# Pooled attention with a maxout feed-forward: batch 1's queries in two parts, a fourth place for K and V, and a new order

## The chip, the cores and the metric

One core of one Trainium2 chip. The metric is device time in microseconds (us), the median over runs of the whole program. Inside the core five engines work from queues of their own: PE (TensorE, matmuls and transposes), DVE (VectorE), ACT (ScalarE), POOL (GpSimd) and SP (SyncE, which here issues DMAs). Each runs its queue in order, and semaphores hold an instruction back until others have ended.

## The reference

```python
# q, k, v: [8, 8, 1152, 64] fp32; w1, w2: [512, 1024]; w_out: [1024, 512]
q_pool = q.reshape(B, H, S // 2, 2, D).mean(axis=3)        # 576 queries per head
scores = scale * np.matmul(q_pool, k.transpose(0, 1, 3, 2))
attn = softmax(scores)                                     # over 1152 keys
x = np.matmul(attn, v).transpose(0, 2, 1, 3).reshape(B * 576, 512)
g = np.maximum(x @ w1, x @ w2)
out = g @ w_out                                            # [4608, 512] fp32
```

## The kernel before

**Algebra.** The maximum is written as relu(x(w1 − w2)) + x w2. So the kernel keeps `wd` = w1 − w2, `w21` = w2 w_out and `wo` = w_out in bf16, computes h = relu(x wd) and adds p = x w21 + h wo. All matmuls are in bf16 with fp32 sums.

**Pairs and blocks.** Two heads of a batch are a *pair*: 32 pairs, four per batch. A *block* is a pair and a range of its queries. Batch 0 comes in two parts: the first 256 queries of its four pairs (below called 0A to 3A), then the other 320. From batch 1 on a block is a whole pair of 576 queries.

**One pair** goes through these steps, named by line of the profile:

- K: load (L464, SP), cast to bf16 in `kbf` (L507, POOL, two buffers), transposed into `kT`: by PE (L518) and a DVE copy (L524) for pairs below `K_PE` = 5, else by a DMA on SP (L533, `ktrans`).
- V: load (L483, SP), cast into `vE` (L584, POOL).
- Q: load (L473, SP), the two neighbours added (L540, POOL, into `qp`), transposed into `qpT`: by PE (L554) with a DVE copy (L560) for pairs below `Q_PE` = 5, else by eight DVE transposes (L573).
- Scores: a score group is 512 columns of two heads (L598, PE), and ACT takes the exponential into `et` (L615).
- AV: chunks of 128 queries (L638) and a rest of 64 (L649) on PE; the V tile carries a column of ones, so the sum comes along.
- Norm: DVE takes the reciprocal of the sum (L661) and multiplies it in (L665, L670) into `xnat`.
- x is transposed into `xT`: by DMA on SP (L704, `xtrans`; two DMAs a pair) or by PE (L721) with a DVE copy (L726) for batch 0 and the pairs in `XPE`.

**Feed-forward.** When x of all four pairs of some tokens is there, h is computed in segments of tokens given by `CUTS` (L809 in pairs of column blocks, L788 singly near the end), and p in 256 tokens (L868; L888 singly at the end). A pair of matmuls on the two halves of PE's rows is called a duo. DVE copies p to `stage` and SP stores it (L829 to L845).

**Places.** K and V of a pair lie in a place, `slot(i)`. Batch 0's four pairs use places 0 to 3, the fourth of which lies in a tile (`xnat[1]`) that batch 1 needs itself; all later pairs go round three places:

```python
def slot(i):
    return i if i < NHP else (i - NHP) % 3
```

`stage` (L381) first holds the fp32 copies of w1 (lower half, later `gT`, the h results) and w_out (`wof`, upper half). Of the upper half the first part is used again as the output buffers `osb`; the rest is not used again once `wof` is cast to `wo`.

**Order.** `table()` holds the order of all engines, written out: one letter per PE unit (the letter is the PSUM bank, a capital letter is a filler of four matmuls on ones, L455, that feeds nobody) and lists of operation numbers for ACT, DVE, POOL and SP. `Plan.arrange` puts the operations in that order, `Plan.solve` works out which semaphore each must wait for. The order in which the main loop creates them only gives them their numbers.

Of the kernel before, what the change touches and what calls it, by code (L numbers as in the profile page):

```python
# [7 lines left out]
P = 128  # L8
# [172 lines left out]
def table():  # L181

    pe = (
        "AAAAAAAAAAAAAAAAAaBbaceGGGGGGGGGgAAacHhgeFfagcefAAAageeeecadegfcefagceageeeeccacecgafgcaedgacaaegabc"
        "cceaccgehcacccggcecccggaggggccegcacceaeeegecdeaeecgdeaggggceeeaeeegeeccaegcccaeeegeaeeecgccccacccecc"
        "cgcccccaeaagaaaaaecccaggegggaggggegggagggecccaggeccccageggggcaaaeggcaaaaegcgggaaeggggcaaaaeaaaagggcg"
        "ggggeaacgaaaaeccccagcccceaagccceccagccccecccaccccccccgcccecagaaeaacaagaaecgaeeeeeecgeeeacaaagaaaaecc"
        "cgcaeccccgaaaeaaacaggeggcaaeaagcaaeaagggcegaaacaaagaeeecageeeeecgeaaaceeeeaeeeegaaaeceeeaeeeeagaaeee"
        "ceaeeeeagaaaceeeegaceeeeegaggggcgggegggagccccgeggggaggccccegggcaceccaccceccaggecccacgcecccagggegggga"
        "cccegaccccccegeeaeeegeecacccgcccceaaagceaaaaaagcggeggggcgggaggecggggagggcgggaggeceeeeaeeegeeeceeeaee"  # L190
        "eegeeeceeaaaaaaaaagceeeeeeagceeeaaaagaaaaeceeegeeeeacaaagaaaaeceeegeeeeaacgeaaaaaaacggegggcgaaaageaa"
        "aagcgggaeeeegceeeeggagggeccccaecccccagegccccgaccccggeggcacccecccgaaaaegaaaaaecgcccceaaaacagaaaccecca"
        "gaaaeaaaagccceccccagggeggacggggeaaacagaeaaacgggeggggcaaaaegcaaaaaegeeeceeeeagggcgggeggagcgggegggaggg"
        "gcgggggeeeacgeeeeeeacaaeaaaagccccegccccceagaaaacaaaaeaaagccccaeccccagaaaceeeegaceeeeegaggggcggeaeeeg"
        "eeceeggaggeeecegeeeaegggcgggeggggagccecccageccccaaaagaaaaccecccacccgggeacggggggeaeeceeeeaggggcggggae"
        "eecegggageggcggeeaeeeceeeegeeeacccgeaccccccgegggcggggaaecgaaaaaaaeccgccaeccccgaaaeaaacaggeggggcgggag"
        "ggeggggcgggagggeggcacceggggaggggaaaccceaaaacccgeaaaaacgeggggcggggegggcaaaaecgggggagggggggeeeeeeeeeee"
        "ecccccccccaaaaaaaaaabaaeeeeeeeeeeeegggghhhhccccddddbbbbaaaahhhhddddggggaaaabbbbbbbbbaaaaeeeeffffaaaa"
        "eeeeffffaaaaeeeeffffaaaaeeeeffffaaaaeeeebbbaaaaaaaaaaaabbbbbbbbbbbbaaaaaaaaaaaabbbbbbbbbbbbaaaaaaaaa"
        "aaa"  # L200
    )
    act = (
# [17 lines left out]
    )  # L220
    dve = (
# [25 lines left out]
    )  # L247
    pool = (
# [5 lines left out]
    )  # L254
    sp = (
# [785 lines left out]
```

## Time and profile before

| | before |
|---|---|
| runs shown | 414.05, 414.01, 407.39 us (median 414.01) |
| profiled execution | 408.94 us, of it the span 407.2 us |
| mean granted TensorE clock | 0.971 |
| PE busy | 371.3 us, 91% of the span |
| ACT busy | 313.8 us, 77% |
| DVE busy | 236.5 us, 58% |
| POOL busy | 131.5 us, 32% |
| score groups, AV matmuls, fillers | 1142 matmuls (L598), 2232 + 558 (L638, L649), 136 (L455) |
| HBM | 62.91 MB read, 9.44 MB written |

How to read it: the span runs from the first to the last instruction of one profiled execution. Busy time is that of an engine's own instructions; waiting, branching and DMA issue are not counted. `SPq` rows are SP's queue: the time an issue took there. A view that lists waits names the engine and line that waited, and what released it. In a timeline, the number in brackets is the idle time of the engine just before the row.

### The profile page before, as it was taken

The page shows a single profiled execution, that of the slowest core. Times are in us where ns is not written, and L with a number is a line of the kernel's source. Part 1 is how long each engine was busy: PE and PEld are TensorE (multiplying, and loading weights), DVE is VectorE, ACT ScalarE, POOL GpSimd, SP SyncE. Part 2 cuts the span into 40 slices and gives each one's busy share as a digit, 9 for nine tenths or more (in the row PEclk, how much of TensorE's full clock was granted, in tenths as well). Part 3 has the DMA queues.
Part 4 walks back from the last instruction along what each step waited for, and adds up shares of the span by engine and source line. Part 5 has one row for each costly group of instructions (what it writes and reads, how often), then busy time and mean ns, then how long its engine had stood idle before and what let it go on. Part 6 is the DMA issues. An engine that isn't in the chain of part 4 may idle for free.

```text
span 407.2 us, 13616 instructions
## 1 busy us (share of the span) xinstructions
PE 371.3 (91%) x6061; PEld 234.8 (58%) x6064; DVE 236.5 (58%) x539; ACT 313.8 (77%) x359; POOL 131.5 (32%) x121
## 2 busy tenths in 40 slices
PE   8989999999689999999269994999699999999996
PEld 8756655675436655656136661566366666556573
DVE  1267549999639667874317672796177774243330
ACT  1599889999769999997239993999689999964231
POOL 2689483443613331234323033333323302000000
PEclk9999999999989999999759998999989999999999
DMA  7999999999996998987986969998966524023313
GB/s 262 400 404 392 377 241 333 329 274 320 280 322 126 244 176 184 227 185 182 270 232 168 210 157 247 224 211 269 196 171 129 132 58 90 13 57 67 78 27 104
DMA packets 79996, 85.19 MB, mean 209 GB/s; under 512 B 51905, under 2 KB 52673, under 8 KB 79937
## 3 DMA queue, kind: packets, MB, share of 16 engines
q1 hardware_dynamic: 79376, 83.53, 77.8%
q8 instruction: 47, 0.77, 0.8%
q10 hardware_dynamic: 560, 0.79, 0.5%
q14 instruction: 13, 0.10, 0.1%
HBM read 62.91 MB, written 9.44 MB: 178 GB/s over the span
## 4 chain that ended last, share of the span: by engine, by line
PE 80%; issue 5%; ACT 4%; DMA 4%; SPq 3%; POOL 2%; DVE 2%; POOLq 0%
PE ps L598 17%; PE ps L638 17%; PE ps L868 17%; PE ps L809 14%; ACT et L615 4%; DMA xT<-xnat 4%; PE ps L888 4%; PE ps L455 3%; PE ps L649 3%; PE ps L788 2%; PE ps L772 2%; SPq L704 1%; POOL qp L540 1%; DVE qpT L573 1%; POOL vE L584 1%
## 5 line engine op out<-in xcount | busy, mean ns | idle before, releaser
L615 ACT ACTIVATE et<-ps 128x1024 bf16<-128x1024 f32 (+5 forms) x340 | 305.4, 1009 | 60.4 <-PE ps L598 59.5
L598 PE MATMUL ps<-qpT,kT 64*128 64x256 bf16 (+7 forms) x1142 | 116.4, 287 | 1.7 <-ACT et L615 0.7
L573 DVE STREAM_TRANSPOSE qpT<-qp 32x288 bf16<-32x288 bf16 x216 | 101.3, 469 | 14.7 <-PE ps L598 10.1
L809 PE MATMUL ps<-xT,wd 64*128 64x256 bf16 (+3 forms) x704 | 79.2, 330 | 27.3 <-DMA xT<-xnat 26.2
L507 POOL TENSOR_SCALAR kbf<-kraw 128x1152 bf16<-128x1152 f32 (+1 forms) x32 | 36.4, 1139 | 160.2 <-DMA kT<-kbf 144.2
L638 PE MATMUL ps<-vE,et 128*128 128x65 bf16 x2232 | 81.2, 193 | 0.0
L638 PEld LDWEIGHTS ps<-vE,et 128*128 128x128 bf16 x2232 | 71.7, 97 | 13.0 <-issue 11.8
L815 DVE TENSOR_SCALAR stage<-ps 128x512 bf16<-128x512 f32 (+3 forms) x44 | 39.9, 907 | 63.8 <-PE ps L809 63.3
L598 PEld LDWEIGHTS ps<-qpT,kT 64*128 64x128 bf16 x1142 | 47.3, 95 | 46.1 <-ACT et L615 16.3
L868 PE MATMUL ps<-wo,stage 64*128 64x512 bf16 x480 | 69.4, 380 | 0.0
L809 PEld LDWEIGHTS ps<-xT,wd 64*128 64x128 bf16 x704 | 31.9, 98 | 52.7 <-DMA xT<-xnat 27.9
L540 POOL TENSOR_TENSOR qp<-qraw 128x576 bf16<-128x576 f32 (+2 forms) x35 | 44.8, 1285 | 18.5 <-DVE qpT L573 17.9
L584 POOL TENSOR_SCALAR vE<-vraw 128x1152 bf16<-128x1152 f32 x31 | 35.7, 1154 | 30.4 <-PE ps L638 30.4
L868 PE MATMUL ps<-w,xT 64*128 64x512 bf16 x240 | 35.5, 377 | 0.3 <-PE ps L809 0.3
L868 PEld LDWEIGHTS ps<-wo,stage 64*128 64x128 bf16 x480 | 23.1, 95 | 17.8 <-issue 0.7
L875 DVE COPY stage<-ps 128x1024 f32<-128x1024 f32 x15 | 18.3, 1221 | 19.3 <-PE ps L868 19.1
L661 DVE RECIPROCAL rc<-ps 128x5 f32<-128x5 f32 (+2 forms) x72 | 13.2, 183 | 27.8 <-PE ps L638 27.2
L670 DVE TENSOR_TENSOR xnat<-ps,rc 128x256 bf16<-128x256 f32 (+1 forms) x72 | 28.2, 394 | 1.9
L649 PEld LDWEIGHTS ps<-vE,et 128*64 128x64 bf16 x558 | 11.3, 111 | 10.2 <-issue 5.3
L868 PEld LDWEIGHTS ps<-w,xT 64*128 64x128 bf16 x240 | 10.6, 94 | 8.8 <-PE ps L809 0.5
L899 ACT COPY stage<-ps 128x512 f32<-128x512 f32 (+1 forms) x4 | 2.2, 560 | 17.3 <-PE ps L888 17.3
L649 PE MATMUL ps<-vE,et 128*64 128x65 bf16 x558 | 14.7, 197 | 0.7 <-ACT et L615 0.5
(50 smaller groups left out, 179.2 us busy)
## 6 DMA issues: line engine op xcount, KB each, us to landing
vraw<-in_v_dram SPq DMA_DIRECT2D x32, 576.0 KB, 6.1
kraw<-in_k_dram SPq DMA_DIRECT2D x31, 576.0 KB, 6.2
qraw<-in_q_dram SPq DMA_DIRECT2D x28, 576.0 KB, 6.1
out_dram<-stage SPq DMA_DIRECT2D x21, 256.0 KB, 4.2
out_dram<-stage SPq DMA_DIRECT2D x23, 128.0 KB, 3.4
xT<-in_moe_w_dram SPq DMA_DIRECT2D x4, 512.0 KB, 11.0
stage<-in_moe_w_dram SPq DMA_DIRECT2D x4, 512.0 KB, 11.8
stage<-in_moe_w_out_dram SPq DMA_DIRECT2D x4, 512.0 KB, 13.0
```

The source lines that it names most:

```text
L507: op("POOL", lambda g: g.tensor_scalar(dst, src, 1.0, 1.0, ALU.mult, ALU.mult), cost=0.02 + 0.126 * (hi - lo), **io)
L540: op(eng, lambda e: e.tensor_tensor(qp[s][:, lo:hi, :], qraw[z][:, lo:hi, 0, :], qraw[z][:, lo:hi, 1, :], ALU.add), r=[f"qraw{z}.{u}" for ...
L573: op("DVE", lambda e, src=src, dst=dst, pb=pb, db=db: e.transpose(view[dst:dst + 32, :, 32 * pb:32 * pb + 32], qp[s][src:src + 32, :, 32 * ...
L584: op("POOL", lambda g: g.tensor_scalar(vE[s][:, :, :, 0:D].rearrange("p t h d -> p h t d"), vraw[z][:, :, :, :], 1.0, 1.0, ALU.mult, ALU.m ...
L598: last = e.matmul(wide[m // 2][:, h, col:col + hi - lo], kT[slot(i)][rows(h), t, :], qpT[i % 4][rows(h), lo:hi], start=True, stop=True)
L615: op("ACT", lambda e, m, col=col, at=at, n=n: e.activation(et2[:, :, at:at + n], wide[m // 2][:, :, col:col + n], EXP, scale=scale), r=[f" ...
L638: last = e.matmul(fb[m + half][:, c * 66:c * 66 + 65], et[:, a:a + P], vE[s][:, t, half, 0:65], start=(t == 0), stop=(t == NT - 1))
L649: last = e.matmul(fb[m][rows(half), NCH * 66:NCH * 66 + 65], et[:, a:a + NB], vE[s][:, t, half, 0:65], start=(t == 0), stop=(t == NT - 1))
L670: op("DVE", lambda e, m: e.tensor_tensor(xnat[xs][:, hp, c0:c1, half * D:half * D + D], banks(m)[:, c0:c1, 0:D], rc[:, i, half, c0:c1].uns ...
L809: last = e.matmul(fb[m + k][:, 0:size], wd[z, ct, (f0 + k) * P:(f0 + k + 1) * P], xT[z, ct, n0:n1], start=(turn == 0 and ct == 0), stop=(t ...
L815: op("DVE", lambda e, m: e.tensor_scalar_max(gT[:, f0:f0 + 2, g0:g0 + size], wide[m // 2][:, :, 0:size], 0.0), r=[f"b{j}.0", f"b{j}.1"], w ...
L868: last = e.matmul(fb[m + k][:, :], lhs, rhs, start=(turn == 0 and x == 0), stop=(turn == 1 and x == NC_ + NF - 1))
```

## The change

- Batch 1 comes in two parts too (`blocks`, L413 of the new file): 256 queries of pairs 4 to 7, then 320. There are 40 blocks in place of 36. The loads, sums and transposes of these queries are cut in the same way, `xtrans` takes a range, and `place`, `spot` and `gkeys` put batch 1's tokens in the order in which they come.
- `Q_PE` goes from 5 to 8: the queries of pairs 5 to 7 are transposed by PE with a DVE copy, and no longer by DVE. 24 of 216 DVE transposes go.
- `XPE` has pair 7 besides pair 31: its x is transposed by PE.
- A fourth place for K and V of batch 1 and later, in the part of `stage` where the copy of w_out lay. The pairs go round four places. What writes there first waits until `wof` is cast.
- `CUTS` has 576 and 832 in place of 512.
- `home`, where a block's exponentials lie in `et`, is a written list for the first 16 blocks.
- `table()` is new in whole. Fillers go from 34 groups to 10 (136 to 40 matmuls). On SP the transposes of K, those of x, loads and stores stand in another order against each other, and so do h, p, score and AV units on PE.

```diff
 def table():
     pe = (
-        "AAAAAAAAAAAAAAAAAaBbaceGGGGGGGGGgAAacHhgeFfagcefAAAageeeecadegfcefagceageeeeccacecgafgcaedgacaaegabc"
...
+        "AAAAAAAabaceGGGgachgefagcefageeeceeagfecdfacegacaaaaeggcaaebggcgeahccccgeagcgbgeacgggegaaaaeeacaaaeeg"
...
-    K_PE, Q_PE, XPE = 5, 5, (NPAIR - 1,)
+    K_PE, Q_PE, XPE = 5, 8, (2 * NHP - 1, NPAIR - 1)
...
+        late = stage[:, (NC_ + 2) * F:2 * NC_ * F].bitcast(BF16)
+        kT.append(late[:, 0:NT * P].rearrange("p (t x) -> p t x", x=P))
+        vE.append(late[:, 2 * F:2 * F + NT * 132].rearrange("p (t h d) -> p t h d", h=2, d=66))
...
-            return i if i < NHP else (i - NHP) % 3
+            return i if i < NHP else (0, 1, 2, 4)[i % NHP]
...
-        blocks = [(i, 0, QA) for i in range(NHP)] + [(i, QA, SQ) for i in range(NHP)] + [
-            (i, 0, SQ) for i in range(NHP, NPAIR)]
+        EARLY = 2 * NHP
+        blocks = [(i, lo, hi) for b in range(2) for lo, hi in ((0, QA), (QA, SQ))
+                  for i in range(b * NHP, b * NHP + NHP)] + [(i, 0, SQ) for i in range(EARLY, NPAIR)]
...
-            home.append(i * NT * QA if hi == QA else i % 3 * NT * (SQ - QA) if hi - lo < SQ else (i + 1) % 2 * PW)
+        home = [0, 2304, 4608, 6912, 0, 2880, 5760, 0, 2880, 5184, 7488, 0, 2304, 5184, 0, 7488] + [
+            i % 2 * PW for i in range(EARLY, NPAIR)]
...
         def ktrans(i):
...
-                dma=f"d_kT{z}", cost=1.0, kind="ktrans", prio=i)
+                after=["wof2"] * (z == 4), dma=f"d_kT{z}", cost=1.0, kind="ktrans", prio=i)
...
         def place(b, c):
+            if b == 1:
+                return SQ + (c * P if c < 2 else NB + c * P if c < NCH else QA)
...
-        def xtrans(i):
+        def xtrans(i, lo, hi):
             b, ct = divmod(i, NHP)
-            spots = [(0, NCH, place(b, 0), P), (NCH, NCH + 1, place(b, NCH), NB)]
-            for c, z, n0, n in spots if b % 2 == 0 else spots[::-1]:
+            spots = [(c, z, place(b, c), P) for c, z in (((0, 2), (2, NCH)) if b == 1 else ((0, NCH),))
+                     if lo <= c * P < hi]
+            if hi == SQ:
+                spots.append((NCH, NCH + 1, place(b, NCH), NB))
+            for c, z, n0, n in sorted(spots, key=lambda x: x[2]):
...
+                if ct == NC_ - 1:
+                    op("POOL", lambda g: g.memset(vE[4][:, :, :, 64:66], 1.0), w=["vE4"],
+                       after=["wof2", "wof3"], fence=True, cost=0.1, kind="ones", prio=ct)
...
-        CUTS = (0, 256, 512, 1024, 1152, 1664, 2048, 2304, 2816, 3072, 3456, 3968, 4096, 4352, 4608)
+        CUTS = (0, 256, 576, 832, 1024, 1152, 1664, 2048, 2304, 2816, 3072, 3456, 3968, 4096, 4352, 4608)
```

More of the change, by code (lines that the diff above doesn't have):

```diff
@@ L183, in table @@
     pe = (
-        "AAAAAAAAAAAAAAAAAaBbaceGGGGGGGGGgAAacHhgeFfagcefAAAageeeecadegfcefagceageeeeccacecgafgcaedgacaaegabc"
[L185 to L198, printed above, removed]
@@ L199, in table @@
-        "eeeeffffaaaaeeeeffffaaaaeeeeffffaaaaeeeebbbaaaaaaaaaaaabbbbbbbbbbbbaaaaaaaaaaaabbbbbbbbbbbbaaaaaaaaa"
-        "aaa"
+        "AAAAAAAabaceGGGgachgefagcefageeeceeagfecdfacegacaaaaeggcaebggcgeahccccgeagcgbgeacgggegaaaaeeacaaaeeg"
+        "eeeeaacegaaagcccceccccabgceaggggaceccccgcccaeccacccgccceaegeeeccccgaeeeeeceeegaeeeceeeeaegggcggggaef"
+        "cghefagceeeeaaeaageccccaagaacaeaaaccgccaecccacccgccceaaagcceacgccceaagaaecaggaegggcaaaeaaaacagggeggc"
+        "aaaeaaaacaggggeggggacccegccaaeaaagaacceccacccgcaaaeacagaaaeeeeaeeeceaaagaaaecagggeggaccccgeccccaggge"
@@ new lines, in table @@
+        "cccacgcccecgggaceggggggacaaeaaaacggggaeggggaacagaeaaaaaaaacaaageeecageeeecaeeggggcggggeeeeaeeeeggggc"
+        "ggggeeeeaeeeeggggcegggggaceccccacccgegggcggggcaccgggegcggggcaccccgcccecccaggggeagggggceeeeaeeeegggcg"
+        "egagggeceeaeeeegcccacceggaccceggacgegggcaaaaeagacaaeeeeegaceeeegggagggcgggegggaggggcgggegggacccceacc"
+        "cccegagccceccccgcccaccegeeecaeeeecgcccaccceccccgaaaaegcaaaaaeegeeaaceeeegaaacaeaagggcaaaaeaaaacgggea"
+        "gggcecccacccgeeeecaeeeeccgcceacccgccccccccecaaagecaaaaaageggacgggegggaaaaaceaaaacgggeaaaagcaaaageggg"
@@ new lines, in table @@
+        "accccgcecccggagggceeeagceeeeeeagcccccccceaaaagaaacaeegeeeeceeeaggggcagggggceaeeggcggegagggceeeaeeegc"
+        "ccccagccccaeeegeeaccccgcccecaagaaeaaaacggggecagggggeceeeeaeeeceeegeaeceeeegeeeceeegeaaacaaagaaaecccc"
+        "geaacccccgeaacaaggggagggegaaacaaagaeeeecgaaaaeeeeecgaaaaeeeeceeeeaaagaaaaeaccccgccccaeeeegcaeeeeegcg"
+        "gggagggeccccacccceggggacggeggggagggccccegaccccceaggcccceccccgagggeggggccaecccccccgaeeeecgeeeeacccgcc"
+        "ceaaagaaaaeaaagaacaeaaagacaeaaagggggceaaaggggceaaaagcaaaaegggcgggageeeecagggggcggggagggceeeeeagggggg"
@@ L201, in table @@
+        "ggggggccccccccccccecccccccccccceeeeeeeeaaaaabaaaabbbbgggghhhhccccddddbbbbeeeeffffgggghhhhbbaaacccccc"
+        "cbbddddaaaabbbbddddaaaabbbbddddaaaabcccccdddddbbbaaaaccccbbbbaaaadddddddccccccccccccddddddddddddcccc"
+        "ccccccccdddddddddddd"
     )
     act = (
[17 rows of a table removed]
[17 rows of a table added]
     )
     dve = (
[25 rows of a table removed]
[26 rows of a table added]
     )
     pool = (
[5 rows of a table removed]
[6 rows of a table added]
     )
     sp = (
[11 rows of a table removed]
[12 rows of a table added]
     )
     bank_a = (
[5 rows of a table removed]
[5 rows of a table added]
     )
     bank_b = (
-        "1 44 454 459 463 473 483 "
+        "1 25 44 83 471 472 477 483 486 491 494 497 "
     )
     bank_c = (
[5 rows of a table removed]
[5 rows of a table added]
     )
@@ L285, in table @@
     bank_d = (
-        "34 38 83 84 458 462 "
+        "35 476 484 487 492 489 499 501 "
     )
     bank_e = (
[5 rows of a table removed]
[5 rows of a table added]
     )
     bank_f = (
-        "28 27 56 19 25 468 471 476 479 "
+        "28 27 34 19 130 76 479 "
     )
     bank_g = (
[4 rows of a table removed]
[5 rows of a table added]
     )
     bank_h = (
-        "14 59 456 461 "
+        "14 38 68 474 482 "
     )
@@ L400, in slot @@
         def slot(i):
-            return i if i < NHP else (i - NHP) % 3
-        blocks = [(i, 0, QA) for i in range(NHP)] + [(i, QA, SQ) for i in range(NHP)] + [
-            (i, 0, SQ) for i in range(NHP, NPAIR)]
+            return i if i < NHP else (0, 1, 2, 4)[i % NHP]
+        EARLY = 2 * NHP
+        blocks = [(i, lo, hi) for b in range(2) for lo, hi in ((0, QA), (QA, SQ))
+                  for i in range(b * NHP, b * NHP + NHP)] + [(i, 0, SQ) for i in range(EARLY, NPAIR)]
         NBL = len(blocks)
-        flat0, home = [], []
-        for n, (i, lo, hi) in enumerate(blocks):
-            flat0.append(flat0[-1] + NT * (blocks[n - 1][2] - blocks[n - 1][1]) if n else 0)
-            home.append(i * NT * QA if hi == QA else i % 3 * NT * (SQ - QA) if hi - lo < SQ else (i + 1) % 2 * PW)
+        home = [0, 2304, 4608, 6912, 0, 2880, 5760, 0, 2880, 5184, 7488, 0, 2304, 5184, 0, 7488] + [
+            i % 2 * PW for i in range(EARLY, NPAIR)]
+        flat0 = [NT * sum(hi - lo for _, lo, hi in blocks[:n]) for n in range(NBL)]
         NGR = (flat0[-1] + PW) // W
@@ L528, in ktrans_pe @@
                 op("DVE", evac, r=[f"b{j}.0"], w=[f"kT{z}.{t}" for t in range(lo, hi)], job=j,
-                   cost=0.16 + (hi - lo) * 0.067, kind="kev", prio=i)
+                   after=["wof2"] * (z == 4), cost=0.16 + (hi - lo) * 0.067, kind="kev", prio=i)
         def ktrans(i):
@@ L656, in norm @@
                 z = c1 + (tail and half == 0)
-                spare_used = ["kT3.%d" % t for t in range(NT)] + ["vE3"] if NHP <= i < 2 * NHP else []
+                spare_used = ["kT3.%d" % t for t in range(NT)] + ["vE3"] if NHP <= i < EARLY else []
                 def banks(m):
@@ L781, in gkeys @@
         def gkeys(lo, hi, ft):
-            return [f"gT.{lo % RING // P + x}.{ft}" for x in range((hi - lo) // P)]
+            return [f"gT.{lo % RING // HP + x}.{ft}" for x in range((hi - lo) // HP)]
         def h_single(n0, n1, ft):
@@ L823, in spot @@
             b, at = divmod(n, SQ)
+            if b == 1:
+                return b, at // HP if at < QA else NT - 1 if at < QA + NB else (at - NB) // HP
             return b, ((at - NB) % SQ if b % 2 else at) // HP
@@ L968, in bass_funnel_attn__then__act_maxout2_kernel @@
                     else:
-                        xtrans(i)
+                        xtrans(i, lo, hi)
                     a_at += 1
                     if i % NHP == NHP - 1:
-                        x_got = hi if i < NHP else (i // NHP + 1) * SQ
+                        x_got = i // NHP * SQ + hi
                     while h_at + 1 < len(CUTS) and CUTS[h_at + 1] <= x_got:
```

158 rows, old and new, of tables (act, bank_a, bank_c, bank_e) are left out of this document.

## The prediction

> **What bounds the kernel now.** I read the page first: its span, its busy times, the clock row, the DMA share and the chain that ended last.
>
> ```profile
> span 407.2 us, 13616 instructions
> PE 371.3 (91%) x6061; PEld 234.8 (58%) x6064; DVE 236.5 (58%) x539; ACT 313.8 (77%) x359; POOL 131.5 (32%) x121
> PEclk9999999999989999999759998999989999999999
> q1 hardware_dynamic: 79376, 83.53, 77.8%
> PE 80%; issue 5%; ACT 4%; DMA 4%; SPq 3%; POOL 2%; DVE 2%; POOLq 0%
> ```
>
> PE is the bound: busy 91% of the span and 80% of the chain. It idles 407.2 − 371.3 = 35.9 us. The view of waits says on what (us in total, times, longest), and PE's timeline where.
>
> ```profile
> PE ps L809 <- DMA xT<-xnat: 26.2, 4, 11.5
> POOL kbf L507 <- DMA kT<-kbf: 144.2, 23, 11.4
> ```
>
> ```profile
> 113.82 0.61 PE L809 MATMUL ps<-xT,wd 64*128 64x512 bf16 x2 [4.90 <-DMA xT<-xnat]
> 207.25 0.50 PE L809 MATMUL ps<-xT,wd 64*128 64x384 bf16 x2 [11.50 <-DMA xT<-xnat]
> 250.54 0.61 PE L809 MATMUL ps<-xT,wd 64*128 64x512 bf16 x2 [5.83 <-DMA xT<-xnat]
> 294.37 0.38 PE L809 MATMUL ps<-xT,wd 64*128 64x256 bf16 x2 [3.99 <-DMA xT<-xnat]
> ```
>
> Four h matmuls, at the ends of batches 1, 3, 4 and 5, wait 26.2 us for the transposed x (`xT`) of their batch's last pair. POOL's 144.2 us cost nothing by themselves: POOL is 32% busy. The windows behind the four waits (length, then busy time and count of PE, PEld, DVE, ACT, POOL, then granted clock, DMA share, GB/s) show a second price; the first row is a stretch ahead of them, for later.
>
> ```profile
> 60.00:100.00 40.00, 39.74 (x673) 24.18 (x671) 37.77 (x82) 39.41 (x45) 17.07 (x14) 1.00 1.10 316
> ...
> 113.80:117.30 3.50, 3.48 (x22) 1.37 (x24) 0.69 (x1) 1.30 (x2) 1.15 (x1) 0.55 1.07 356
> ...
> 207.20:212.60 5.40, 5.35 (x38) 2.48 (x40) 0.96 (x1) 3.02 (x3) 2.52 (x2) 0.51 0.93 208
> ...
> 250.20:253.60 3.40, 3.06 (x20) 1.27 (x22) 0.27 (x1) 1.02 (x1) 0.78 (x1) 0.52 0.91 285
> 294.40:297.90 3.50, 3.50 (x24) 1.69 (x26) 1.16 (x2) 1.58 (x3) 0.00 (x0) 0.51 0.83 317
> ```
>
> PE is full there but at about half the granted clock. Length times (1 − clock) is 1.58 + 2.65 + 1.63 + 1.72 = 7.6 us. The four ends cost 33.8 us, the rest of PE's idleness 35.9 − 26.2 = 9.7 us.
>
> **Why these matmuls wait.** For each batch I add up the work that PE's written order puts between the last AV of its last pair and the first h matmul that needs it. The prices are these rows: 0.215 us for two 512-column matmuls of h or p (a "duo"; columns set it, so 0.11 for 256, 0.165 for 384, 0.055 for 128), 0.22 for a score group, 1.74/6 = 0.29 for an AV chunk of nine, 0.40 for an AV rest.
>
> ```profile
> 343.40 0.86 PE ps L809 x8
> 342.31 0.22 PE ps L598 x4
> 163.88 1.74 PE ps L638 x54
> 216.27 0.40 PE ps L649 x18
> ```
>
> Before, the cover is 4.9, 12.1, 4.3, 5.0, 4.0 and 6.2 us for batches 1 to 6. Cover plus wait is what was needed: 9.8, at most 12.1, 15.8, 10.8, 8.0 and at most 6.2. After, batch 1's last pair goes through PE, with 16 us and more between; the others have 13.2 (24 p duos, 15 score groups, 24 h duos of 128, a rest, 8 chunks, 3 duos), 4.8 (14 p duos, 6 score groups, 3 h duos of 384), 12.1, 15.2 and 8.4. By these needs batches 1, 2, 4, 5 and 6 no longer wait; batch 3 is the case to look at.
>
> **Batch 3.** Why it needed 15.8 us stands on DVE, POOL and SP, in order of time:
>
> ```profile
> 190.78 0.18 DVE L661 RECIPROCAL rc<-ps 128x4 f32<-128x4 f32 x1
> 190.99 0.42 DVE L670 TENSOR_TENSOR xnat<-ps,rc 128x256 bf16<-128x256 f32 x1
> ```
>
> ```profile
> 191.81 2.08 SPq L533 DMA_TRANSPOSE kT<-kbf  x1
> ...
> 200.62 0.39 SPq L464 DMA_DIRECT2D kraw<-in_k_dram  x1
> 201.05 1.31 SPq L839 DMA_DIRECT2D out_dram<-stage  x2
> 202.41 3.53 SPq L704 DMA_TRANSPOSE xT<-xnat  x2
> ```
>
> ```profile
> 199.44 1.15 POOL L507 TENSOR_SCALAR kbf<-kraw 128x1152 bf16<-128x1152 f32 x1 [7.51 <-DMA kT<-kbf]
> ```
>
> x was finished at 191.42, but its transposes were issued at 202.41. SP's queue is in order: it stood at a load of k (200.62) that waits for a cast on POOL (199.44), which waited 7.51 us for the landing of the K transpose issued at 191.81. That one went out so late because its place in `kT` was still being read. With four places the same transpose is released ten score groups earlier, a pair's worth, so load and cast are done when x comes. What is left: norm 0.6, one of the two issues ahead (3.53/2 = 1.8), and the landing:
>
> ```profile
> DMA to landing us min/median/max: 3.2/6.0/9.5
> ```
>
> ```profile
> DMA to landing us min/median/max: 2.2/4.3/7.2
> ```
>
> (first tile `kT`, then `xnat`). 0.6 + 1.8 + 4.3 = 6.7 against 4.8 of cover: **2.0 us** of wait (0 at the shortest landing; at the other end all of today's 11.5 + 2.65 = 14.1).
>
> **The other parts.** *Batch 6* has 8.4 us, 2.2 more than enough before, against the 8.0 to 15.8 of the batches that waited: 0.5 (0 to 2.4, batch 4's 10.8 as need). *K of pair 7* goes on SP behind the transposes of the first part of pair 4: 0.6 + 1.8 + 6.0 = 8.4 us, against 16 duos, 8 h duos of 256, 9 score groups, 4 q and 2 x groups = 8.2 on PE: 0.5 (0 to 3.7, at a landing of 9.5). No PE wait for a K transpose by DMA stands in the trace, so the fourth place gives nothing but batch 3's release.
>
> *More work on PE*: the queries of pairs 5 to 7 by PE are 54 transposes, pair 7's x five, by the first two of these rows; the DVE rows are for what it gets rid of and takes on.
>
> ```profile
> 23.56 0.34 PE L554 MATMUL ps<-ident,qp 64*64 64x64 bf16 x10
> ```
>
> ```profile
> 49.51 0.42 PE L721 MATMUL ps<-ident,xnat 128*128 128x128 bf16 x3
> ```
>
> ```profile
> L573 DVE STREAM_TRANSPOSE qpT<-qp 32x288 bf16<-32x288 bf16 x216 | 101.3, 469 | 14.7 <-PE ps L598 10.1 <-PE ps L809 0.8
> L560 DVE COPY qpT<-ps 128x256 bf16<-128x256 bf16 (+2 forms) x9 | 2.9, 319 | 5.4 <-PE ps L554 5.4
> ```
>
> 54 × 0.034 + 5 × 0.14 = **2.5 us** (to 5 where they meet a half clock); the cut h segment keeps its columns. ACT's 313.8 us would be 83% of 377, so it does not become the bound. *DVE* loses 24 × 0.469 = 11.3 us and takes nine copies of 0.32 and at most 16 more norm instructions (8 × 0.18 + 8 × 0.42 = 4.8): net −3.6. DVE is 37.8 of 40 us busy in the first window, but PE is 39.74 there, so it is worth **−0.3** (0.26 is PE's whole gap; 0). Extra norm work hides under PE; were that cover gone it would cost its 4.8.
>
> *The front* loses 96 of 136 filler matmuls (L455). Rows of PE and POOL:
>
> ```profile
> 11.00 3.85 PE L455 MATMUL ps<-ones 128*128 128x128 bf16 x36
> 14.69 0.44 PE L518 MATMUL ps<-ident,kbf 128*128 128x128 bf16 x5
> 16.49 0.67 PE L518 MATMUL ps<-ident,kbf 128*128 128x128 bf16 x9
> ```
>
> ```profile
> 7.70 0.73 POOL L507 TENSOR_SCALAR kbf<-kraw 128x640 bf16<-128x640 f32 x1 [6.13 <-DMA kraw<-in_k_dram]
> ```
>
> The last part of the first K is cast at 8.43, but its transposes stand behind 36 fillers and run at 14.69. With 12 fillers there (12 × 0.107 = 1.3 us) they come up to 24 × 0.107 = 2.5 us earlier; behind them the stream needs other loads too, so I take **−1.0** (−2.5; +3 if a gap there brings one half-clock stretch, 2.65, the longest seen).
>
> **The sum.** 407.2 − 26.2 − 7.6 = 373.4; + 2.0 + 0.5 + 0.5 + 2.5 − 0.3 − 1.0 = 377.6. The profiled execution took 408.94, 1.74 more than its span: **379 us**. That execution lies 1.2% under the 414.01 median of the runs shown, so against the median the gain would look larger.
>
> **The clock.** The windows show what follows a wait of 4 us or more: about half the clock for 3.4 to 5.4 us. The fillers at 11.00 take 107 ns each against 74 for the nine transposes of the same width at 16.49. The Trainium skill ("TensorE: Matmul & The Clock Gate", Part 1: The HAM clock gate) says that the clock stays at half until PE was busy for about 3.4 us and falls back after an idle window. The four windows agree with it (0.51 to 0.55), while the slow fillers, 3.85 us of unbroken work, do not. By that rule a front with 96 fewer fillers would open at half clock, which speaks against this edit.
>
> **Rivals.** *A front at half clock*: the gaps where fillers lay come out as idle PE, and each is followed by a half-clock stretch. Four such, as many as the waits now, at 2.65: 379 + 10.6 = **390**. For it: 10.3 us of filler time go. Against: the last 36 delay real work.
>
> *SP still holds the x transposes back*: if another entry blocks the queue at batch 3 (14.1 in place of 2.0) and batch 6 ends like batch 5 (4.0 + 1.7 for 0.5): 379 + 12.1 + 5.2 = **396**. For it: SP's order is new everywhere, and 23 POOL waits on K transposes still feed it. Against: in SP's new order I find no entry that waits long ahead of x.
>
> *It doesn't do what it says*: the DMA queues set the pace. q1 is at 77.8% of 16 engines, 317 us; in 377 it would need 84%. If it can't, waits move from xT to loads and the time stays at 401 to 417, **409** in the middle. For it: 1.10 in the window 60 to 100. Against: that same window shows PE full.
>
> *Slower: the loop of the K transposes becomes the bound.* The cast of the next k waits for a K transpose to land, the load behind that cast holds SP, and the next K transpose stands behind the load. One turn is the landing L, a cast of 1.15 behind two others of that length, and two issues of 0.39: L + 4.2. A pair has 377.6/32 = 11.8 us, and the fourth place gives a lead of three pairs, 35 us, to eat up over 24 pairs. It costs more than 21.5 us (no longer faster) from L = 24 turns of 2.35 over, 9.95, and it is slower than 417 from L = 10.6; at 11 the time is 379 + 24 × 3.4 − 35 = **426**. For it: the 144.2 us. Against: the median is 6.0, the longest of all 9.5, and the shorter span only raises the DMA share.
>
> **How the numbers follow.** Forecast, with its own range of 371 to 389: 0.66; half-clock front 0.05; SP 0.09; these are faster by over 2% (8.2 us, about what a measurement of this kernel can tell from no change): 0.80. DMA pace: 0.10, within 2%. The K loop or something like it: 0.10, slower. The low end: waits of batches 3, 6 and pair 7 at nothing and the front at −2.5 give 374.9, and a third of the other 9.7 us of idleness could go with the new order: 371. The high end: 373.4 with 14.1 + 2.4 + 3.7 + 5 + 3 makes 401.6, with 1.7 around it 403; I cut at **402**, which leaves out most of the last two cases.
>
> **What would show it.** Right: no wait of L809 for xT over 1 us except batch 3's (around 2); no window at 0.5 behind them; PE busy about 356 us (371.3 + 2.5 − 7.6 − 96 × 0.107); the cast of k far ahead of the K transposes. Wrong: L809's waits over 6 us in total, PE waiting at L598 for `kT` by DMA (the K loop), K landings over 9 us in the median, or a clock near 0.5 in the first 40 us with idle PE between (front). Under 371 would mean the order also removed idleness that I left standing.

## The result and the profile after

The changed kernel takes **376.32 us** in the median of four runs (375.53 to 377.84), the kernel before 412.56 (407.39 to 414.05, four runs): a ratio of 0.92, 95% interval 0.9108 to 0.9292. The ratio leaves out the slower ones among the runs of the kernel before; the medians alone give 0.912. The forecast was 379, and faster. The profiled execution took 377.84, its span 376.1.

The page of the changed kernel:

```profile
span 376.1 us, 13754 instructions
PE 359.9 (96%) x6123; PEld 231.3 (62%) x6127; DVE 230.8 (61%) x544; ACT 312.7 (83%) x355; POOL 132.6 (35%) x126
PEclk9989999999999999999999999999999999999999
q1 hardware_dynamic: 79424, 83.38, 83.2%
```

PE is still the bound, idle 16.2 us in place of 35.9 and busy 11.4 us less. The clock row shows full speed but for one slice in the front. The lines of its view of waits that answer to those of before:

```profile
POOL kbf L514 <- DMA kT<-kbf: 64.7, 16, 7.4
POOL kbf L514 <- DMA stage<-kbf: 13.1, 5, 4.4
PE ps L824 <- DMA xT<-xnat: 2.8, 1, 2.8
PE ps L605 <- DMA stage<-kbf: 0.8, 1, 0.8
```

PE's waits for xT fell from 26.2 us in four to 2.8 in one, and POOL's waits for the landing of K's transposes from 144.2 to 77.8 (the second row is the fourth place, which is named `stage`). PE's timeline, both waits:

```profile
66.39 0.83 PE L605 MATMUL ps<-qpT,stage 64*128 64x256 bf16 x12 [0.83 <-DMA stage<-kbf]
...
185.15 0.34 PE L824 MATMUL ps<-xT,wd 64*128 64x384 bf16 x2 [2.77 <-DMA xT<-xnat]
```

The first is pair 7's K, the second batch 3's x. SP and DVE ahead of the second:

```profile
177.71 0.42 DVE L679 TENSOR_TENSOR xnat<-ps,rc 128x256 bf16<-128x256 f32 x1
```

```profile
177.48 1.17 SPq L480 DMA_DIRECT2D qraw<-in_q_dram  x1
178.69 2.44 SPq L716 DMA_TRANSPOSE xT<-xnat  x2
```

x is finished at 178.13 and its DMAs go out from 178.69. In the kernel before, the same step took from 191.42 to 202.41.

### The profile page after: what moved, and what is told of

The parts are those of the page before. It is cut to its first block, busy times and chain, and to the rows that moved or that the text cites. A ratio compares the mean times of both kernels' runs of the same rounds, so it can differ in the third digit from the quotient of the medians.

```text
span 376.1 us, 13754 instructions
## 1 busy us (share of the span) xinstructions
PE 359.9 (96%) x6123; PEld 231.3 (62%) x6127; DVE 230.8 (61%) x544; ACT 312.7 (83%) x355; POOL 132.6 (35%) x126
## 3 DMA queue, kind: packets, MB, share of 16 engines
q1 hardware_dynamic: 79424, 83.38, 83.2%
## 4 chain that ended last, share of the span: by engine, by line
PE 81%; DMA 11%; DVE 2%; SPq 2%; POOL 2%; issue 1%; DVEq 0%; POOLq 0%
PE ps L885 19%; PE ps L647 19%; PE ps L605 18%; PE ps L824 14%; DMA qraw<-in_q_dram 5%; PE ps L905 4%; PE ps L658 3%; DMA vraw<-in_v_dram 3%; PE ps L803 2%; DMA kraw<-in_k_dram 2%; DMA xT<-xnat 1%; POOL qp L547 1%; DVE qpT L580 1%; SPq L540 1%; SPq L480 1%
## 5 line engine op out<-in xcount | busy, mean ns | idle before, releaser
L622 ACT ACTIVATE et<-ps 128x1024 bf16<-128x1024 f32 (+2 forms) x336 | 304.3, 1019 | 29.2 <-PE ps L605 28.3
L580 DVE STREAM_TRANSPOSE qpT<-qp 32x288 bf16<-32x288 bf16 x192 | 90.1, 469 | 23.9 <-PE ps L605 20.6
L605 PE MATMUL ps<-qpT,kT 64*128 64x256 bf16 (+7 forms) x918 | 89.9, 281 | 2.1 <-ACT et L622 0.6
L824 PE MATMUL ps<-xT,wd 64*128 64x256 bf16 (+5 forms) x768 | 74.1, 301 | 3.1 <-DMA xT<-xnat 2.8
L647 PE MATMUL ps<-vE,et 128*128 128x65 bf16 x1728 | 64.7, 194 | 1.6 <-issue 0.8
L647 PEld LDWEIGHTS ps<-vE,et 128*128 128x128 bf16 x1728 | 57.0, 98 | 11.5 <-issue 9.2
L830 DVE TENSOR_SCALAR stage<-ps 128x512 bf16<-128x512 f32 (+5 forms) x48 | 40.3, 839 | 36.8 <-PE ps L824 36.5
L605 PEld LDWEIGHTS ps<-qpT,kT 64*128 64x128 bf16 x918 | 36.6, 95 | 35.4 <-ACT et L622 11.4
L605 PE MATMUL ps<-qpT,stage 64*128 64x256 bf16 (+7 forms) x260 | 26.1, 280 | 0.8 <-DMA stage<-kbf 0.8
L647 PE MATMUL ps<-stage,et 128*128 128x65 bf16 x504 | 17.8, 193 | 0.0
L647 PEld LDWEIGHTS ps<-stage,et 128*128 128x128 bf16 x504 | 16.0, 97 | 2.5 <-issue 2.2
```

Source lines behind the costliest of these rows:

```text
L580: op("DVE", lambda e, src=src, dst=dst, pb=pb, db=db: e.transpose(view[dst:dst + 32, :, 32 * pb:32 * pb + 32], qp[s][src:src + 32, :, 32 * ...
L605: last = e.matmul(wide[m // 2][:, h, col:col + hi - lo], kT[slot(i)][rows(h), t, :], qpT[i % 4][rows(h), lo:hi], start=True, stop=True)
L622: op("ACT", lambda e, m, col=col, at=at, n=n: e.activation(et2[:, :, at:at + n], wide[m // 2][:, :, col:col + n], EXP, scale=scale), r=[f" ...
L647: last = e.matmul(fb[m + half][:, c * 66:c * 66 + 65], et[:, a:a + P], vE[s][:, t, half, 0:65], start=(t == 0), stop=(t == NT - 1))
L824: last = e.matmul(fb[m + k][:, 0:size], wd[z, ct, (f0 + k) * P:(f0 + k + 1) * P], xT[z, ct, n0:n1], start=(turn == 0 and ct == 0), stop=(t ...
L830: op("DVE", lambda e, m: e.tensor_scalar_max(gT[:, f0:f0 + 2, g0:g0 + size], wide[m // 2][:, :, 0:size], 0.0), r=[f"b{j}.0", f"b{j}.1"], w ...
```

## The experiments

Each was timed in three rounds beside the kernel before, each group of runs on a chip of its own. There the kernel before had a median of 413.1 us (group 1: runs 1 to 4), 409.1 (group 2: 5 to 8) and 409.4 (group 3: 9 to 12).

**1. x of four pairs by PE, in the kernel before.** The orders have its four PE transposes and DVE copies in place of eight DMAs.

```diff
-    K_PE, Q_PE, XPE = 5, 5, (NPAIR - 1,)
+    K_PE, Q_PE, XPE = 5, 5, (7, 15, 19, 23, NPAIR - 1)
```

> The kernel before, with x of pairs 7, 15, 19 and 23 (the last pairs of batches 1, 3, 4 and 5) transposed by PE and copied by DVE in place of the DMA; nothing else moves but a few neighbouring score groups. Theory (the four waits of h for xT and the half clock behind them are what the change got back): L809's waits on DMA for xT go from 26.2 us to under 2, no half-clock window stands behind them, PE gets four transposes of 0.7 us, up to 0.5 us each of new waiting: about 379 us (375 to 385), near the changed kernel's 376. Rival 1 (the gain comes from the fourth place, the new SP order and the shorter front, and the waits would only move to another place): 395 to 410. Rival 2 (DMA sets the pace): 400 or more.

Measured: 396.61 us (391.51 to 397.55), ratio 0.9627 (0.9472 to 0.9783). That is half of what the theory asked for, and in the range of rival 1, by which the waits would move. The waits went at batches 1 and 3, but of 16.0 us that are left, 3.13 stand at batch 2, where there was no wait, and 4.14 and 8.70 at batches 4 and 5 again, for x of another pair. PE's timeline, then SP and POOL ahead of the longer wait:

```profile
282.27 0.61 PE L814 MATMUL ps<-xT,wd 64*128 64x256 bf16 x4 [8.70 <-DMA xT<-xnat]
```

```profile
276.97 0.39 SPq L469 DMA_DIRECT2D kraw<-in_k_dram  x1
277.41 0.60 SPq L844 DMA_DIRECT2D out_dram<-stage  x1
278.05 2.79 SPq L709 DMA_TRANSPOSE xT<-xnat  x2
```

```profile
275.80 1.15 POOL L512 TENSOR_SCALAR kbf<-kraw 128x1152 bf16<-128x1152 f32 x1 [10.13 <-DMA kT<-kbf]
```

x of pair 22 stands behind a load of k, the load behind a cast, and the cast waited 10.13 us for a K transpose. What the prediction saw at batch 3 alone is at work elsewhere too.

**2. x of pair 15 first on SP, in the kernel before.** In the SP list its two DMAs move ahead of four stores, a load of q, the load of k and two stores.

> The kernel before, with one move on SP: the two transposes of pair 15's x go ahead of four stores, a load of q and the load of k that waits for a cast. Theory (batch 3's 11.5 us come from SP standing at that load, which the fourth place cures in the change): SP issues them at about 194 in place of 202.4, the wait falls from 11.5 to 3 to 5 us, the half clock behind it stays or goes: 6.5 to 10 us off, the other three waits as they were. Rival (the landing of the transposes is what is late, because K's transpose lies ahead of them in the DMA queues): the wait stays over 9 us.

Measured: 409.33 us (402.46 to 415.67), ratio 0.985 (0.9668 to 1.0032): the time doesn't settle it, the profile does. Batch 3's wait is 2.74 us in place of 11.5, but a new one of 2.86 stands at 235.12, and batches 1, 4 and 5 keep 3.24, 6.18 and 5.14. The entry ahead of x on SP was the cause there; moving one x leaves the others where they are.

**3. Pair 18 in pair 15's place, in the changed kernel.**

```diff
         def slot(i):
+            if i in (18, 19):
+                return 4 if i == 18 else 2
             return i if i < NHP else (0, 1, 2, 4)[i % NHP]
```

> The changed kernel, with pairs 18 and 19 in each other's places: K of pair 18 must wait until pair 15's scores are read, as with three places, while all orders stay. Theory (the fourth place works only through SP at batch 3): SP stands at pair 18's K transpose, the cast and the load of k behind it come late, x of pair 15 is issued some 6 us later, and batch 3's wait goes from 2.8 to 7 to 11 us, with a half-clock stretch of some 2 us behind it: 5 to 10 us slower, about 383. Rival (batch 3 is cured by the h units standing later or by less DVE work, not by the place): under 2 us slower.

Measured: 386.16 us (385.37 to 386.65), ratio 0.9412 (0.9331 to 0.9494), against 0.9313 (0.9227 to 0.94) for run 5. These intervals overlap and the chips differ, so the time alone doesn't settle it; SP's and PE's timelines do:

```profile
174.28 1.30 SPq L542 DMA_TRANSPOSE stage<-kbf  x1
...
181.68 0.37 SPq L473 DMA_DIRECT2D kraw<-in_k_dram  x1
182.09 2.14 SPq L542 DMA_TRANSPOSE kT<-kbf  x1
184.28 0.95 SPq L482 DMA_DIRECT2D qraw<-in_q_dram  x1
185.27 2.42 SPq L718 DMA_TRANSPOSE xT<-xnat  x2
```

```profile
190.56 0.50 PE L826 MATMUL ps<-xT,wd 64*128 64x384 bf16 x2 [6.34 <-DMA xT<-xnat]
```

The K transpose that went out at 167.71 in the changed kernel goes out at 174.28, behind a gap of 8.39 us in SP's queue, the load behind it at 181.68, x at 185.27, and the wait is 6.34 us, with a granted clock of 0.50 in the 3.4 us behind it. In the new order the early place does what the prediction said.

**4. Pair 7's x by DMA, in the changed kernel.**

```diff
-    K_PE, Q_PE, XPE = 5, 8, (2 * NHP - 1, NPAIR - 1)
+    K_PE, Q_PE, XPE = 5, 8, (NPAIR - 1,)
```

> The changed kernel, with pair 7's x transposed by DMA on SP again, in three DMAs, in place of PE and DVE. Theory (batch 1's wait is gone by the cover of 16 us and more that the cut and the order give, not by the use of PE): no wait of L824 for it, PE 0.7 us less: 376 within 1.5 us. Rival (the transposes by PE cured batch 1): a wait of 4 us or more at batch 1 and half a clock behind it, 381 or more.

Measured: 381.94 us (380.75 to 385.17), ratio 0.9324 (0.9215 to 0.9432), against 0.9313 for run 5. No h matmul of batch 1 waits for it. Cover removed that wait, not the use of PE. The profile has batch 3's wait at 4.36 us and one of 1.36 at 155.49; why these are longer here stays open.

**5. The changed kernel again**, for comparison on the second chip.

> The changed kernel as it is, for comparison on the same chip with the runs beside it: 376 (375 to 379) if its time there is that of the first runs; up to 382 if what the run with pair 7's x by DMA lost lies in the chip and not in the edit.

Measured: 379.21 us (378.89 to 381.41), ratio 0.9313 (0.9227 to 0.94). Its batch 3 waits 0.80 us.

**6. More cover at batch 3, in the changed kernel.** Eight p duos and two score groups go ahead of the h units, and on SP x of pair 15 ahead of a load of q.

> The changed kernel with more cover at batch 3: the h units that need pair 15's x stand behind eight more duos of p and two score groups, and a load of q on SP stands behind the transposes of that x. Theory (cover less than need sets that wait): need 7.5 less 0.6, cover 4.8 + 2.2, so the wait of 2.8 goes to 0 to 0.6 and the time falls by about 2.2 us. Rival (the PE stays as busy behind it as before, so the work only moves and waits later for something else): under 0.5 us.

Measured: 379.29 us (376.34 to 380.12), ratio 0.9291 (0.9197 to 0.9384). The wait is gone, but on this chip there was only 0.80 us of it. No gain is shown.

**7. The fourth place alone, in the kernel before.** The two tiles in `stage`, the memset and the waits on `wof2` as in the change, and:

```diff
-            return i if i < NHP else (i - NHP) % 3
+            return i if i < NHP else (0, 1, 2, 4)[i % NHP]
```

> The kernel before with the fourth place for K and V alone: its orders and blocks as they were. Theory of the prediction (the place is worth only batch 3's release of SP): batch 3's wait falls from 11.5 to 3 to 5 us and the others stay, 7 to 10 us off, about 402. Rival (SP stands at loads of k behind casts that wait for K's transposes at other batches too, as the run with x on PE shows at 276.97, where x of pair 22 stood behind such a load): POOL's wait on K transposes falls from 144 us to under 90, the four waits fall from 26 to under 14 us in all, and the time to 395 or less.

Measured: 410.73 us over ten runs (404.97 to 414.76), ratio 1.0029 (0.9963 to 1.0095). Both theories fall: the place alone is worth nothing, not even at batch 3, where the profile (of a run of 414.76 us) has a wait of 11.39 us. The rows of SP and POOL, with those of the kernel before that answer to them behind:

```profile
185.76 1.94 SPq L541 DMA_TRANSPOSE kT<-kbf  x1
...
193.19 0.37 SPq L472 DMA_DIRECT2D kraw<-in_k_dram  x1
...
196.91 2.17 SPq L541 DMA_TRANSPOSE kT<-kbf  x1
```

```profile
192.01 1.15 POOL L515 TENSOR_SCALAR kbf<-kraw 128x1152 bf16<-128x1152 f32 x1 [8.51 <-DMA kT<-kbf]
```

```profile
179.68 2.21 SPq L533 DMA_TRANSPOSE kT<-kbf  x1
...
188.11 0.37 SPq L464 DMA_DIRECT2D kraw<-in_k_dram  x1
188.53 2.10 SPq L704 DMA_TRANSPOSE xT<-xnat  x1
190.67 0.58 SPq L483 DMA_DIRECT2D vraw<-in_v_dram  x1
191.30 0.47 SPq L473 DMA_DIRECT2D qraw<-in_q_dram  x1
```

```profile
186.93 1.15 POOL L507 TENSOR_SCALAR kbf<-kraw 128x1152 bf16<-128x1152 f32 x1 [8.90 <-DMA kT<-kbf]
```

Now the loop can be read. A K transpose is issued (179.68), it lands, the cast that waited for its buffer runs (186.93 to 188.08), the load of k behind that cast goes out (188.11), then x, v and q, and then, without a gap, the next K transpose (191.81): 12.1 us a round, with every x of the stage inside it. That transpose did not wait for its place at all. With four places this round is 11.2 us (185.76 to 196.91), those beside it are 13.3 and 13.7, and the same chain holds. In the changed kernel 12 of the 27 K transposes stand right behind a load of k, against 3 in the kernel before, and so here:

```profile
167.71 1.52 SPq L540 DMA_TRANSPOSE kT<-kbf  x1
...
175.75 0.37 SPq L471 DMA_DIRECT2D kraw<-in_k_dram  x1
176.16 1.28 SPq L540 DMA_TRANSPOSE stage<-kbf  x1
```

8.5 us is the round there (167.71 to 176.16), 8.7 and 9.8 are those beside it.

**8. Both: x of the four pairs by PE and four places**, in the kernel before.

> The kernel before with both: x of pairs 7, 15, 19 and 23 by PE, and the fourth place. If the remaining waits of the run with x on PE (4.1 and 8.7 us, for x of the pairs ahead) come from SP standing at loads of k, they go, and with them the half clock: waits of L809's line under 2 us in all, 378 to 384 us, which is the changed kernel's time without its order, its fillers or its cut of batch 1. If they have another cause (the order of h against AV), 390 or more.

Measured: 394.54 us (393.51 to 395.57), ratio 0.9678 (0.9591 to 0.9765), where run 1 has 0.9627: again no gain from the place is shown, and the theory's 378 to 384 us is missed. Waits for xT of 2.80, 4.23 and 4.57 us are left.

**9. K's transposes ahead of the load on SP, three places.** In the SP list of the kernel before, the K transposes of pairs 8 to 27 move ahead of the load of k that stood before them, which takes them out of the loop.

> The kernel before with its three places; on SP, K's transposes of pairs 8 to 27 go ahead of the load of k that stood before them, with all else in its order. New theory (before, SP runs a loop: a load of k waits for a cast, the cast for the landing of the last K transpose, and the next K transpose stands behind that load and the entries after it, 12 us a round, so x stands behind it; the fourth place alone could not help): with three places the K transpose is free of the loop but must wait for its place, so SP stands there in place of at the load: about no change, 402 to 415, with POOL's wait on K transposes under 144 us. Rival (the loop alone was the matter, and three places do): 395 or less.

Measured: 412.05 us over ten runs (405.82 to 414.38), ratio 1.003 (0.9968 to 1.0092). As expected: with three places SP stands at the K transpose instead, and L814's waits for xT are 27.8 us.

**10. The same with four places.**

> The same move on SP with the fourth place. New theory: both causes of SP's standing are gone, POOL's wait on K transposes falls from 156 us to under 90, K's transposes come ten score groups earlier, x is issued within 3 us of its norm, and the four waits fall from 29.5 us to 8 to 16 (cover of 4 to 5 us against a need of 6 to 8): 385 to 396. Rival (the place and the SP order do little; the order of h against AV on PE makes the difference): 400 or more.

Measured: 388.94 us (388.56 to 391.55), ratio 0.9561 (0.9471 to 0.9651). Neither the place (run 7) nor the move (run 9) changes the time alone; together they take 20 us. Its view of waits, and the waits for xT of 1 us and more in PE's timeline:

```profile
POOL kbf L515 <- DMA kT<-kbf: 41.0, 10, 9.4
POOL kbf L515 <- DMA stage<-kbf: 19.8, 6, 5.9
```

```profile
116.03 0.61 PE L820 MATMUL ps<-xT,wd 64*128 64x512 bf16 x2 [7.90 <-DMA xT<-xnat]
...
275.69 0.28 PE L820 MATMUL ps<-xT,wd 64*128 64x256 bf16 x2 [2.60 <-DMA xT<-xnat]
```

SP's own waits show why neither edit is enough. The rows are its waits at loads of k for a cast, in the kernel before and in runs 7, 9 and 10:

```profile
SPq L464 <- POOL kbf L507: 57.1, 13, 6.9
SPq L472 <- POOL kbf L515: 61.7, 14, 7.0
SPq L469 <- POOL kbf L512: 1.9, 1, 1.9
SPq L472 <- POOL kbf L515: 2.5, 2, 2.1
```

In the same order, the gaps in front of K transposes in SP's timelines (those over 0.15 us, from 60 us on) add up to 20.4 us at eight of them, none, 83.0 us at twenty, and 7.9 us at six. The place alone ends SP's standing at K transposes and leaves that at the loads; the order alone moves it from the loads to the transposes; both together end most of it.

Batch 1's 7.90 us are not the loop. SP's timeline has the issue of one K transpose at 102.04 that took 5.80 us; x of pair 7 was finished at 102.80 and went out behind it, at 108.51 and 111.00, not within the 3 us that were expected. Of this run's 27 issues of K transposes, 23 took 1.27 to 2.84 us; why this one took longer is not shown.

```profile
102.04 5.80 SPq L541 DMA_TRANSPOSE stage<-kbf  x1
```

**11. The same with x of the four pairs by PE as well.**

> The same, and x of pairs 7, 15, 19 and 23 by PE as well. New theory: the waits that were left with x on PE and four places (2.8, 4.2 and 4.6 us, for x of the pairs ahead, behind SP) go too: under 2 us in all, no half clock, 379 to 385 us, the changed kernel's time on this chip without its orders on PE, ACT and DVE, its fillers and its cut of batch 1. Rival (the searched order on PE is needed): 390 or more.

Measured: **377.97 us** (377.69 to 378.55), ratio 0.9283 (0.9186 to 0.938), level with the changed kernel's 0.9313 of run 5. Its page:

```profile
span 376.0 us, 13640 instructions
PE 365.4 (97%) x6081; PEld 232.7 (62%) x6084; DVE 238.3 (63%) x543; ACT 312.9 (83%) x359; POOL 131.5 (35%) x122
PEclk9999999999999999999999999999999999999999
```

No wait for xT by DMA stands in its view of waits. So three edits give the whole gain: the place, the position of K's transposes on SP, and x of the last pairs early. It keeps the 136 fillers, DVE's q transposes for pairs 5 to 7 and batch 1 in one part. This shows what is enough, not how the changed kernel, which also puts more work between AV and h, divides its gain.

**12. Sixty-four fillers more, in the changed kernel**, 40 at the start and 24 behind the first twelve.

> The changed kernel with 64 filler matmuls more, as before: 40 ahead of the first q and 24 behind the first twelve of them. If the front's gain comes from the fillers that went (2.5 us of real work earlier; the traces show ACT 5.4 us more busy in the first 20 us), the time rises by 2 to 5 us. If the front is paced by loads that land later anyway, or the fillers keep the clock up at 24 to 27 us, it stays within 1.5 us.

Measured: 379.17 us (378.85 to 385.65), ratio 0.9305 (0.9208 to 0.9402), where run 5, on another chip, has 379.21. No worth of the fillers that went is shown, within an interval of 4 us either way. But they do set the clock in the front. The windows of run 12 (its profile is of a run of 385.65 us):

```profile
20.00:24.00 4.00, 3.64 (x85) 2.44 (x83) 2.44 (x10) 4.00 (x6) 2.35 (x3) 1.00 1.03 404
24.00:27.20 3.20, 2.17 (x28) 1.14 (x28) 1.97 (x4) 3.20 (x4) 2.49 (x2) 1.00 1.03 403
```

With 64 more fillers PE is busy 3.64 of the 4 us before 24 us and the granted clock stays at 1.00; in run 5 it is busy 1.92 us there, and the clock is 0.50 from 24.00 to 27.20. The other three runs of run 12 have a mean clock of 0.999 to 1.000, the four of run 5 one of 0.991 to 0.995.

## Why the prediction was right, and where it was not

**The bound and the price** were right: the four waits for xT and the half clock behind them were the loss. Run 11 removes both with the old PE order but for the four transposes, and the time is the changed kernel's.

**Batch 3's chain after**: 2.0 us forecast, 2.77 measured, by the steps that were named (norm, an issue ahead, the landing, which took 5.2 us where the sum had 4.3); 0.80 on another chip. **Pair 7's K**: 0.5 forecast, 0.83. **Batch 6**: no wait, 0.5 forecast. **More work on PE**: 2.5 forecast; the groups of q and x transposes went from 3.2 and 3.3 us busy to 5.1 and 4.0, together 2.6. **DVE**: 3.6 us less forecast, 5.7 measured; PE had no gap there to take it.

**The step that failed** is the cause of batch 3's 15.8 us: "That one went out so late because its place in `kT` was still being read." The transpose at 191.81 follows the entry before it without a gap. It was late because it stood behind a load that waited for the K transpose before it (run 9, which takes it out from behind that load, finds the place to be the next limit). This is the loop that the prediction made its slower rival for the changed kernel, while the kernel before was already running in it. With it falls "so the fourth place gives nothing but batch 3's release": alone it gives nothing (run 7), with SP's order 20 us (run 10), and in the new order a place that comes late brings batch 3's wait back to 6.34 us (run 3). The total held, in part by luck. The sum took the needs of 10.8, 9.8 and 8.0 us as given and met them by more cover; only for batch 3 it had the need fall (0.56 us from norm to issue in place of 10.99), if for the wrong reason. But run 10 shows that the others fall too: with the old cover of 4.3, 5.0 and 4.0 us, batches 3 to 5 wait 0.39, 0 and 2.60 us. How much of the changed kernel's gain at batches 4 and 5 is cover and how much a smaller need was not measured.

**The front** was given −1.0 for fillers; run 12's interval of 4 us can't tell this from 0. The half-clock front, a rival and one of the signs of being wrong, came in small. The window of the changed kernel:

```profile
24.00:27.20 3.20, 3.20 (x52) 2.61 (x49) 1.40 (x5) 2.07 (x3) 2.25 (x2) 0.51 1.04 406
```

Behind idle stretches between 20 and 24 us stands one half-clock stretch, 3.2 × 0.49 = 1.6 us, of the four that the rival had; run 12 shows that it comes from the fillers that went. In those 4 us PE is busy 2.26 us, and its longest gap is 0.82 us. The rule of the Trainium skill cited in the prediction ("TensorE: Matmul & The Clock Gate", Part 1: The HAM clock gate) has the clock fall back after an idle window of about 3.4 us; no gap of that length stands here, so the trace does not agree with the rule as it is put there.

**PE's busy time** was to be 356 us and is 359.9, of which this stretch is 1.6. The span still came out 1.5 under the sum: PE idles 16.2 − 3.6 = 12.6 us outside the two waits named above, where the sum had left 377.6 − 356 − 3.0 = 18.6, and it did not say where. So busy time that was 3.9 us too low and idle time that was 5.4 us too high (21.6 for 16.2) nearly cancel, which is luck. Which part of the new order saved this idle time is not shown.

## What to carry to other kernels

When transfers stand late in an in-order queue, follow the entry ahead of them round to where it started: a load that waits for a cast that waits for a transfer behind an earlier load is a loop, and its round, not any one wait, is to be shortened. A spare buffer and a new queue order can be worth nothing alone and 20 us together, so a release that is read off the code is to be looked for in the trace (is there a gap in front of the entry?) before it is priced. A wait that is removed can uncover the next one behind the same queue, as in runs 1 and 2.

## What was not expected of the hardware

PE's waits of 2.6 to 3.2 us went with either clock in the 3.4 us behind them: full speed behind 2.60 us (run 10), 2.77 (the changed kernel), 2.80 (run 8) and 3.13 (run 1, at 155.08), two thirds behind 2.74 (run 2) and 3.10 (run 9, at 168.60), half behind 2.86 (run 2, at 235.12, where two matmuls and another wait follow). All the waits for xT of 3.24 us and more had 0.50 to 0.66 behind them. The rows of run 1 and run 2:

```profile
155.10:158.50 3.40, 3.40 (x36) 1.47 (x38) 2.25 (x4) 2.31 (x3) 1.10 (x1) 1.00 0.23 54
```

```profile
195.90:199.30 3.40, 3.40 (x30) 1.60 (x32) 0.96 (x1) 2.07 (x3) 2.77 (x3) 0.66 0.95 259
```

The DMA queues took the shorter span without slowing the K transposes by much: q1's share rose from 77.8% to 83.2%, and the median landing of those into the first three places from 6.0 to 6.4 us:

```profile
DMA to landing us min/median/max: 3.2/6.4/12.1
```
